# An attention and channel-mix kernel on one core: the tail tokens' load moved ahead of w_k, 82 filler products, new orders for three engines

## The chip, the core and the metric

The kernel runs on one core of one Trainium2 chip. The metric is the device time of one execution in microseconds (us). Five engines matter. TensorE (PE) multiplies and transposes into PSUM; a product is a weight load (PEld) and a matmul. ScalarE (ACT) does exponentials, relu, tanh, and many copies out of PSUM. VectorE (DVE) does the elementwise work and the other copies. GpSimd (POOL) issues the loads that cast float32 to bfloat16; SyncE (SP) issues the first loads of q, the stores of the output, and transposing DMAs. Each engine works through its own list in order and waits on semaphores for the others.

## What is computed

```python
scores = scale * q @ k.T                     # 8 batches, 8 heads, 576 tokens, head size 64
scores = where(0 <= rel < 128, scores - slope[h] * rel, -1e9)    # rel = row - column
attn   = softmax(scores) @ v
x      = attn, heads side by side            # 8 x 576 x 512
xk, xr = mu * x + (1 - mu) * x_prev          # x_prev: x one token earlier; mu_k and mu_r
k      = relu(xk @ w_k)                      # 512 x 1024
out    = sigmoid(xr @ w_r) * ((k * k) @ w_v) # 1024 x 512
```

Products take bfloat16 and add up in float32; the output is float32.

## The kernel before

**Tiles.** A batch's 576 tokens are four blocks of 128 and a tail of 64 (`LAST`). The heads go in four groups `g` of two. Batches go in pairs `P`: the channel mix runs over the 1152 tokens of a pair in four blocks, which I call a (tokens 0 to 511 of the pair, for pair 0 split into a, 0 to 255, and b, 256 to 511), c (512 to 895) and d (896 to 1151).

**The order of the work is written out.** `Plan.add` takes every operation of the program with what it needs; those of PE, ACT and DVE are numbered in the order in which the program adds them. `ORDER` (from L19) holds, for each of the three engines, the list of these numbers in which it does them. Where an operation may run on ACT or on DVE (copies of qk, some squares), the list that holds its number decides. `Plan.run` steps through a model of the machine to choose buffers and to merge all queues, but within PE, ACT and DVE the lists are followed. GpSimd's loads keep the order in which the program makes them; for batch 0, the weights and batch 1 that is the string `LOADS`, a letter for each step of `load_step`: v (the first half of batch 0's v), 2 (q and k of batch 0, tokens 256 to 511, to `part_buf`), K and k (the halves of w_k), t (the tail tokens' q and k, to `ts`, in `tail_load`, L534), V (the second half of v, and its tail `tv`), a, b, c (batch 1's q and k, its tail, its v), R (w_r), W and w (the halves of w_v).

**The operations by name.** On PE, for batch 0 and group g: Tg transposes q and k of tokens 0 to 255 (loaded by SP and ACT in float32, cast by DVE for groups 0 and 1, transposed as float32 for groups 2 and 3); Bg writes the bias into PSUM as a product (L748); Sg adds the scores (L742); Ag multiplies by v (L395); Xg transposes the attended output (L398). With a prime they belong to the second part, tokens 256 to 575; qg are its transposes of q and k, t0 those of the tail tokens (L395, `ident,ts`), M that of mu. For batch b from 1 on: qb.g, Sb.g (twice, for two halves), Ab.g, Xb.g (two groups at once), tb; the bias is there a multiplication by a mask on DVE (L779). In the mix, KPxf is the product with 128 columns of w_k for block x of pair P, RPxc that with w_r for 128 tokens, VPxc one half (four of eight parts) of that with w_v. W is a filler: a product of zeros by zeros (`emit_warm`), 90 of them (`NWARM`), which nobody reads.

Behind a T, q or t stands a copy from PSUM (L715, ACT or DVE); behind S the exponential on ACT (L766); behind A the division on DVE (L813, L819); behind X a copy on ACT (L715), then the difference and the two mixes xk and xr on DVE (L906, L913); behind K a relu on ACT (L1022) and a square on DVE or ACT (L996, L994); behind R a tanh on ACT (L1040); behind the second V the output product on DVE (L1054) and the store.

PE's list from its start to the first product of a mix after those of pair 0's blocks a and b, by these names:

```
Wx34 B3 B0 B2 Wx23 T0 Wx11 S0 T3 Wx6 B1 W T2 S3 Wx4 T1 Wx4 M A3 W S2 A0 Wx4 q1 S1 q3 A2 B3' W X3 q2 A1 S3' q0
B0' W X0 X1 B2' X2 S2' t0 S0' B0' B3' B2' S3' S0' B1' S2' B1' S1' A0' A3' S1' K0a4 A2' X0' K0a6 A1' K0a0 K0a2
K0a1 X1' q1.1 X2' K0a5 X3' K0a7 K0a3 q1.2 q1.0 S1.1 K0b5 t1 K0b1 R0a1 R0a0 S1.1 S1.0x2 V0a0 V0a1 q1.3 S1.2
V0a0 S1.2 S1.3 V0a1 S1.3 K0b3 K0b6 K0b2 A1.0 A1.2 A1.1 A1.3 K0b0 R0b2 X1.0 K0b4 q2.1 K0b7 V0b2 R0b3 q2.2 X1.2
t2 V0b3 S2.1x2 S2.2 V0b3 V0b2 q2.0 q2.3 S2.2 K0d3
```

The functions that the change touches:

Of the kernel before, what the change touches and what calls it, by code (L numbers as in the profile page):

```python
# [20 lines left out]

ORDER = {
    "PE": [int(x) for x in """
# [17 lines left out]
""".split()],  # L41
    "ACT": [int(x) for x in """
# [11 lines left out]
""".split()],  # L54
    "DVE": [int(x) for x in """
# [16 lines left out]
""".split()],  # L72
}

# [168 lines left out]
def kernel(  # L243
# [32 lines left out]
    XB = range(4, B)  # L276
    XO = range(6, B)
    X0 = 16
    NWARM = 90
    LOADS = 'v2KtVkabRWwc'  # L280
    XD = 4
    OTL = 1.5
    FIN = 384
# [328 lines left out]
    def load_step(what):  # L612
        if what in "vV":
            if what == "v" and VCUT:
                n_w["d"] = pool_op(0.55, emit_cut, [n_ident])
            for j in ((0, 1) if what == "v" else (2, 3)):
                vl[0].append(v_load(0, j, vh[0], [gv[0]] + blank_v + (
                    src0[1, VDEP - 1] if VDEP and j == 0 else [])))
                if j == 0 and not VCUT:
                    n_w["d"] = pool_op(0.55, emit_cut, [n_ident, last[POOL]])  # L620
                    last[POOL] = n_w["d"]
            if what == "V":
                vl[0].append(tv_load(0, vh[0], blank[0:4]))
        elif what in "23":
            if what == "2":
                src1[0] = src1[1] = [run_load(lambda: part_buf, i, 0, 256, 2, 0, H) for i in range(2)]
        elif what == "t":
            th[0], tl[0] = tail_load(0)
        elif what in "Kk":
            j = int(what == "k")  # L630
            n_w["k", j] = w_load(wk_sb[:, :, 512 * j:512 * j + 512],
                                 moe_w_k[:, 512 * j:512 * j + 512], 820 + 210 * (1 - j))
        elif what == "R":
            n_w["r"] = w_load(wr_sb, moe_w_r, 840)
        elif what in "Ww":
            j = int(what == "w")
            n_w["v", j] = w_load(wv_sb[:, 4 * j:4 * j + 4], moe_w_v[512 * j:512 * j + 512], 820)
        elif what in "abc":
            batch_load(1, what)
# [33 lines left out]

    for what in LOADS:
        load_step(what)
# [32 lines left out]
    g_wm = plan.add(VIR, 0.0001, 0.0001, [], (0,), None, [h_wm])  # L708
    for i in range(NWARM):
        plan.add(PE, 0.118 if i < 40 else 0.056, 0.0, [n_warm, g_wm], (1e12, i), emit_warm, (), [h_wm])  # L710
# [613 lines left out]
```

## Time and profile before

| | |
|---|---|
| time, median of 3 runs | 228.89 us (228.83 to 229.37) |
| the profiled execution | 228.23 us, span 226.2 us |
| PE busy | 218.4 us, 97% of the span |
| DVE busy | 186.3 us, 82% |
| ACT busy | 156.2 us, 69% |
| POOL busy (issuing loads) | 92.1 us, 41% |
| fillers | 90, from 1.0 to 15.6 us |
| granted PE clock | 0.998 |

The span runs from the first to the last instruction in the profile. Matmuls are pipelined, so one's length (some 0.2 us for the shortest) is longer than the time until the next can start, and PE can count as busy while it does little. A row of a timeline gives the start, the length of a run of like instructions, what they write and read, their count, and in brackets the idle time before them and what ended it. A row of the chain of waits gives start, length, engine and line. Where an engine's waits name a DMA, that load had landed just before.

### The profile page before, as it was taken

What the parts mean: (1) busy time and instruction counts of PE and PEld (TensorE: products, weight loads), DVE (VectorE), ACT (ScalarE), POOL (GpSimd) and SP (SyncE); (2) the same over time, 40 slices, a digit from 0 to 9 for tenths busy, and PEclk for the clock granted to TensorE, in tenths of its full rate; (3) what the DMA queues carried; (4) which work ended last, traced back from release to release, by engine and by line L of the source; (5) the groups of instructions that cost most, each with busy time, mean ns of one, the idle gap of its engine ahead of it and who ended that gap; (6) DMA issues with size and microseconds to landing.
All of it is one profiled execution on the core that took longest, in us unless ns stands there. A gap on an engine that the chain in (4) does not pass through costs nothing.

```text
span 226.2 us, 6452 instructions
## 1 busy us (share of the span) xinstructions
PE 218.4 (97%) x2572; PEld 132.6 (59%) x2603; DVE 186.3 (82%) x418; ACT 156.2 (69%) x284; POOL 92.1 (41%) x118
## 2 busy tenths in 40 slices
PE   8999999999999999999999999999999999999994
PEld 7766855756666555555666554556665564655442
DVE  7388979899879999988989969969989999834153
ACT  2489999899999876877497198665697644545121
POOL 8956727599971973396258610330000000000000
PEclk9999999999999999999999999999999999999999
DMA  6999999999999999999999999799811083202026
GB/s 169 180 185 199 197 195 177 224 149 155 182 171 165 98 194 173 197 170 151 206 183 128 155 188 179 155 114 239 154 31 32 36 158 64 90 3 80 17 96 229
DMA packets 129981, 33.19 MB, mean 147 GB/s; under 512 B 116632, under 2 KB 126112, under 8 KB 129952
## 3 DMA queue, kind: packets, MB, share of 16 engines
q0 software_dynamic: 95728, 16.26, 100.6%
q1 hardware_dynamic: 32480, 15.94, 33.5%
q10 hardware_dynamic: 1744, 0.59, 1.1%
q8 instruction: 20, 0.33, 0.6%
q14 instruction: 9, 0.07, 0.1%
HBM read 33.56 MB, written 9.44 MB: 190 GB/s over the span
## 4 chain that ended last, share of the span: by engine, by line
PE 78%; ACT 12%; DMA 3%; DVE 3%; issue 2%; DVEq 0%; ACTq 0%
PE duo L395 68%; PE duo L742 6%; ACT at L766 3%; PE duo L398 3%; DMA out_dram<-ot 3%; ACT qk L715 3%; ACT xt L715 2%; ACT rl L1022 2%; ACT mask L1198 1%; DVE ot L1054 1%; PE duo L748 1%; ACT kk L994 1%; DVE xu L819 1%; DVE kk L996 0%; ACT rs L1040 0%
## 5 line engine op out<-in xcount | busy, mean ns | idle before, releaser
L395 PE MATMUL duo<-xk,wk_sb 128*128 128x256 bf16 (+2 forms) x413 | 71.0, 313 | 0.5 <-ACT rl L1022 0.2
L766 ACT ACTIVATE at<-duo 128x1024 bf16<-128x1024 f32 (+2 forms) x68 | 64.4, 1008 | 8.4 <-PE duo L742 8.3
L395 PE MATMUL duo<-wv_sb,kk 128*128 128x512 bf16 (+2 forms) x279 | 68.5, 373 | 1.3 <-issue 0.6
L1022 ACT ACTIVATE rl<-duo 128x256 bf16<-128x256 f32 (+2 forms) x104 | 47.6, 499 | 26.2 <-PE duo L395 20.9
L395 PEld LDWEIGHTS <-wk_sb 128*128 128x128 bf16 x416 | 38.9, 97 | 23.8 <-issue 1.6
L779 DVE TENSOR_TENSOR at<-at,mask 128x1024 bf16<-128x1024 bf16 x56 | 37.9, 686 | 7.1 <-ACT at L766 6.7
L395 PEld LDWEIGHTS <-kk 128*128 128x128 bf16 x296 | 26.8, 98 | 27.4 <-issue 0.9
L519 POOL DMA_DIRECT2D vs<-in_v_dram x32 | 28.5, 909 | 32.5 <-PE duo L395 30.9
L996 DVE TENSOR_TENSOR kk<-rl 128x256 bf16<-128x256 bf16 (+2 forms) x92 | 29.6, 336 | 10.8 <-ACT rl L1022 10.1
L1040 ACT ACTIVATE rs<-duo 128x512 bf16<-128x512 f32 x36 | 22.3, 628 | 22.5 <-DVE ot L1054 15.1
L395 PE MATMUL duo<-wr_sb,xr 128*128 128x512 bf16 x133 | 34.9, 379 | 0.6
L1054 DVE SCALAR_TENSOR_TENSOR ot<-rs,duo 128x512 f32<-128x512 bf16 (+2 forms) x37 | 24.3, 664 | 9.3 <-PE duo L395 5.7
L819 DVE TENSOR_TENSOR xu<-duo,rc 128x640 bf16<-128x640 f32 (+2 forms) x36 | 26.6, 745 | 0.4
L913 DVE SCALAR_TENSOR_TENSOR xr<-dl,mu_sb,xt 128x576 bf16<-128x576 bf16 (+1 forms) x32 | 24.9, 779 | 0.0
L913 DVE SCALAR_TENSOR_TENSOR xk<-dl,mu_sb,xt 128x576 bf16<-128x576 bf16 (+1 forms) x32 | 24.5, 778 | 0.1
L395 PEld LDWEIGHTS <-at 128*128 128x128 bf16 x576 | 21.3, 97 | 5.5 <-issue 0.9
L395 PEld LDWEIGHTS <-xr 128*128 128x128 bf16 x144 | 13.8, 98 | 14.5 <-issue 0.4
L395 PE MATMUL duo<-vs,at 128*128 128x65 bf16 x512 | 21.8, 193 | 0.0
L550 POOL DMA_DIRECT2D cb<-in_k_dram x20 | 17.8, 930 | 4.9 <-DMA vs<-in_v_dram 4.4
L550 POOL DMA_DIRECT2D cb<-in_q_dram x20 | 17.8, 942 | 1.4 <-DMA cb<-in_k_dram 1.4
L715 ACT COPY xt<-duo 128x640 bf16<-128x640 bf16 (+3 forms) x28 | 15.6, 593 | 2.4 <-PE duo L398 2.4
L715 ACT COPY qk<-duo 128x512 bf16<-128x512 bf16 (+1 forms) x26 | 15.1, 605 | 2.6 <-PE duo L398 2.6
(73 smaller groups left out, 189.0 us busy)
## 6 DMA issues: line engine op xcount, KB each, us to landing
out_dram<-ot SPq DMA_DIRECT2D x30, 256.0 KB, 4.7
vs<-in_v_dram POOLq DMA_DIRECT2D x32, 128.0 KB, 7.9
cb<-in_q_dram POOLq DMA_DIRECT2D x20, 128.0 KB, 9.5
cb<-in_k_dram POOLq DMA_DIRECT2D x20, 128.0 KB, 10.8
out_dram<-ot SPq DMA_DIRECT2D x10, 128.0 KB, 1.8
wk_sb<-in_moe_w_k_dram POOLq DMA_DIRECT2D x2, 512.0 KB, 8.7
cb<-in_q_dram POOLq DMA_DIRECT2D x4, 256.0 KB, 8.7
cb<-in_k_dram POOLq DMA_DIRECT2D x4, 256.0 KB, 8.9
```

What stands on the lines that cost most here:

```text
L395: return use(h, nc.tensor.matmul(*a, **k))
L519: return dma(POOL, 256, issue_t(1024), lambda e: nc.gpsimd.dma_start(out=vs_buf[h.idx][:, j, :, 0:D], in_=v[b, :, 128 * j:128 * j + 128].r ...
L550: return [dma(POOL, 256, issue_t(1024), lambda e, r=r: nc.gpsimd.dma_start(out=cb_buf[h.idx][:, i, r], in_=src[:, :, r]), [g], kind="q") f ...
L715: return (nc.scalar.copy if e == ACT else nc.vector.tensor_copy)(out=out, in_=in_)
L766: lambda e, ah=ah, w=w, hp=hp: nc.scalar.activation(out=ah(), in_=two(hp)[:, :, 0:w], func=AF.Exp, scale=float(scale)), (), [hp])
L779: nc.vector.tensor_tensor(out=a, in0=a, in1=m, op=ALU.mult)
L819: use(hp, nc.vector.tensor_tensor(out=out_, in0=a5()[:, :, :, 0:D], in1=rc[:, :, 0:nt, None].to_broadcast([128, 2, nt, D]), op=ALU.mult), hx)
L913: lambda e: nc.vector.scalar_tensor_tensor(out=buf[hk.idx][:, g, e0 + c0:e0 + c1], in0=dls(), scalar=mu[:, g:g + 1], in1=xc(1), op0=ALU.mu ...
L996: nc.vector.tensor_tensor(out=out, in0=in_, in1=in_, op=ALU.mult)
L1022: a = op(ACT, act_t(n), [s], pr, lambda e, hp=hp, hr=hr: use(hp, nc.scalar.activation(out=rl_buf[hr.idx][:, 0:n], in_=one(hp)[:, 0:n], fun ...
L1040: lambda e, hp=hp, hs=hs: use(hp, nc.scalar.activation(out=rs_buf[hs.idx], in_=one(hp), func=AF.Tanh, scale=0.5), hs), [hs], [hp])
L1054: use(hv, nc.vector.scalar_tensor_tensor(out=ot_buf[ho.idx][:, a:b], in0=rs_buf[hs.idx][:, a:b], scalar=1.0, in1=one(hv)[:, a:b], op0=ALU. ...
```

## The change

Three things change. The letter t moves ahead of K in `LOADS`. `NWARM` goes from 90 to 82; since the fillers are numbered 39 to 128 before and 39 to 120 after, every later operation's number falls by 8, and nearly every number in the lists changes for that alone. And all three lists are new.

```diff
 ORDER = {
     "PE": [int(x) for x in """
-40 113 74 125 85 56 118 80 117 109 43 51 42 89 121 63 103 88 49 92 96 66 94 48 119 127 126 68 100 55 101 110 107
...
+105 79 88 117 91 107 56 92 89 98 78 102 101 66 110 49 69 104 67 58 115 53 51 114 50 84 68 93 119 57 112 87 54 99
...
     "ACT": [int(x) for x in """
-10 11 12 13 14 132 135 158 173 146 161 207 149 240 178 223 244 189 140 154 258 166 227 193 261 247 196 260 262
...
+10 11 12 13 127 14 165 153 141 170 232 233 158 132 215 199 198 219 146 202 236 205 239 185 188 222 251 255 249
...
     "DVE": [int(x) for x in """
-0 2 4 8 3 9 7 6 5 1 35 32 36 33 30 28 34 27 26 25 29 31 129 130 143 21 23 18 17 16 19 22 144 15 20 24 170 38 175
...
+0 1 4 34 30 5 28 35 27 2 33 25 36 3 32 121 122 31 29 6 135 16 18 19 136 124 23 7 138 21 9 24 26 15 162 150 8 17
...
@@ -276,8 +276,8 @@
     X0 = 16
-    NWARM = 90
-    LOADS = 'v2KtVkabRWwc'
+    NWARM = 82
+    LOADS = 'v2tKVkabRWwc'
     XD = 4
```

The new PE list by the names above, over the same stretch:

```
Wx45 T0 Wx5 B3 W B0 W T1 Wx5 S0 Wx3 T3 W T2 Wx3 B2 W S3 W S2 A0 Wx2 A3 Wx2 B1 A2 Wx2 S1 W X3 M Wx3 q3 B2' W X2
A1 X0 q2 Wx3 q0 q1 S2' W t0 W B1'x2 X1 S1' B3' S3' S1' B0' B3' S3' S0' B0' A1' B2' S0' S2' A3' K0a0 A0' X1'
K0a5 K0a3 A2' K0a7 X3' K0a4 q1.1 K0a2 X0' K0a1 X2' K0a6 q1.0 q1.3 q1.2 S1.1 t1 K0b5 K0b4 R0a1 R0a0 S1.3 S1.0
S1.2 V0a0 V0a1 S1.1 S1.0 V0a0 V0a1 S1.2 S1.3 K0b2 K0b3 K0b1 K0b7 A1.0 A1.1 K0b0 A1.3 R0b2 A1.2 X1.0 q2.1 K0b6
R0b3 V0b2 X1.2 q2.2 S2.1 V0b3 t2 S2.2 V0b2 q2.3 q2.0 V0b3 S2.1 S2.2 K0c3
```

Thirteen operations go from ACT to DVE: the copies behind T0, T1 and T2, one of the two behind q0, q1.0, q1.3 and q2.3, and the squares behind K0a2, K0a4, K0a6, K0c1, K0c6 and K0c7. Six go from DVE to ACT: one copy behind each of q1, q3, q1.3 and q2.0, and the squares behind K0b6 and K0c5. In DVE's new list the two output products of V0a stand together ahead of the masks of S1.0, S1.2 and S1.3 (second halves); in the old list one of them stood ahead of both of S1.2's and the other ahead of S1.3's. ACT's new list makes all eight exponentials of batch 0's second part before the first of the eight mask rows (L1198); the old one has four mask rows among them. The rest of the lists, to the end, is reordered in the same manner; both end with R3d8 between the parts of V3d8.

82 rows, old and new, of the table ORDER are left out of this document.

## The prediction

> **What bounds the kernel now.** I read the page first, then busy time by stretch, then the chain of waits in order of time, and last the timelines of TensorE (PE), ScalarE (ACT), VectorE (DVE) and GpSimd (POOL) over the first 55 us. Engine rows and stretches (start:end, length, busy time and count of each engine, granted clock, DMA share, GB/s):
>
> ```profile
> span 226.2 us, 6452 instructions
> PE 218.4 (97%) x2572; PEld 132.6 (59%) x2603; DVE 186.3 (82%) x418; ACT 156.2 (69%) x284; POOL 92.1 (41%) x118
> 5.00:10.00 5.00, 4.93 (x65) 3.87 (x63) 2.47 (x9) 1.45 (x3) 5.00 (x8) 1.00 1.89 182
> 10.00:20.00 10.00, 9.73 (x206) 6.33 (x202) 7.65 (x25) 9.29 (x21) 6.21 (x10) 1.00 1.58 192
> 25.00:30.00 5.00, 4.40 (x130) 3.49 (x117) 4.96 (x13) 5.00 (x16) 2.78 (x4) 1.00 1.29 207
> 30.00:52.00 22.00, 21.74 (x408) 13.19 (x412) 19.49 (x41) 20.86 (x39) 14.56 (x19) 1.00 1.91 183
> 52.00:223.00 171.00, 168.57 (x1650) 97.68 (x1675) 143.04 (x290) 113.35 (x196) 56.47 (x68) 1.00 1.29 134
> ```
>
> From 52 to 223 us PE is busy 168.57 of 171.00 us: 2.43 us of it is idle, and a new order can win no more than that there. The real room lies ahead of 30 us, where "busy" hides fillers and short tiles. There ACT is the full engine (9.29 of 10, then 5.00 of 5), with DVE at 4.96 of 5 beside it. The early steps, first from the chain of waits (start, length), then from the timelines:
>
> ```profile
> 0.99 3.32 PE duo L395 x34
> 4.31 0.98 PE duo L748 x6
> 5.29 1.28 PE duo L395 x23
> 6.57 0.24 PE duo L398 x4
> 7.47 0.34 PE duo L742 x4
> ```
> ```profile
> 7.74 0.66 PE L398 MATMUL duo<-id,qx 128*128 128x128 f32 x4
> 28.34 0.40 PE L742 MATMUL duo<-qk 64*128 64x256 bf16 x4 [0.45 <-ACT qk L715]
> 29.44 0.38 PE L398 MATMUL duo<-ident,ts 128*128 128x128 bf16 x4 [0.16 <-ACT qk L715]
> 30.09 1.89 PE L395 MATMUL duo<-wr_sb,xr 128*128 128x512 bf16 x7
> ```
> ```profile
> 7.85 0.81 ACT L766 ACTIVATE at<-duo 128x768 bf16<-128x768 f32 x1 [0.43 <-PE duo L742]
> 13.25 0.82 ACT L766 ACTIVATE at<-duo 128x768 bf16<-128x768 f32 x1
> ```
>
> The first transposes of q and k (T0) start only when 57 fillers and three bias pairs are through; the exponentials of its four groups of heads then run from 7.85 to 14.1. From there to R0a, the first w_r product at 30.09, PE twice waits for ACT's copies of qk (0.45 and 0.16): ACT's backlog sets the start of R0a. What R0a also needs is w_r itself. The load's issue, its time to landing, and what GpSimd's waits say of other loads:
>
> ```profile
> 18.14 0.81 POOL L560 DMA_DIRECT2D wr_sb<-in_moe_w_r_dram  x1
> 29.66 0.76 POOL L515 DMA_DIRECT2D cb<-in_q_dram  x1 [1.44 <-DMA wr_sb<-in_moe_w_r_dram]
> 14.59 0.74 POOL L515 DMA_DIRECT2D cb<-in_k_dram  x1 [1.87 <-DMA wk_sb<-in_moe_w_k_dram]
> 34.79 0.74 POOL L515 DMA_DIRECT2D cb<-in_q_dram  x1 [1.84 <-DMA wv_sb<-in_moe_w_v_dram]
> ```
> ```profile
> wr_sb<-in_moe_w_r_dram POOLq DMA_DIRECT2D x1, 512.0 KB, 11.2
> ```
>
> 18.14 + 11.2 = 29.3 us. So R0a starts 0.7 us behind its weights, and the loads, which follow one another in one queue, are a floor close under the present schedule.
>
> **The change, part by part.** *Tail tokens ahead of w_k.* Only the letter t moves, past K; v stands ahead of K before and after, and V, the later half of v, behind it, so the "v" of the title is no change. The tail loads and the first scores that want them:
>
> ```profile
> L534 POOL DMA_DIRECT2D ts<-in_q_dram x1: 565/565/565, 6.7 to 6.7; - x1
> DMA to landing us min/median/max: 7.7/7.8/7.9
> 16.83 0.65 PE L395 MATMUL duo<-ident,ts 64*64 64x32 bf16 x32
> 21.40 0.61 PE L395 MATMUL duo<-xk,wk_sb 128*128 128x256 bf16 x4
> ```
>
> The tails land at about 6.7 + 7.7 = 14.4 and 14.9 and are used at 16.83. In front of w_k's 512 KB they land earlier by what these take: as an estimate 2.2 to 2.6 us, the 1.44 to 1.87 us that GpSimd waits on a load of that size and its own issue of 0.75 between; so near 12. The two tails together are a quarter of that size (64 KB each), so w_k's first half is put back by 0.6 us, from just under 14.59 to some 15; its first user is at 21.40, and the 6 us between hide that. No later load changes place. Price of the move: 0; if that cover were gone, 0.6 us.
>
> *82 fillers for 90.* Fillers run only where PE has nothing else. 23 take 1.28 us, 56 ns each, so eight are 0.45 us, all of it ahead of 17 us in time that PE waits for loads or ACT anyway: 0 by itself. What counts is the place: 45 fillers now stand ahead of T0, not 57 with three bias pairs. The first 34 end at 4.31, eleven more at 4.31 + 11 x 0.056 = 4.92, so T0 ends at 5.16, not 6.81.
>
> *The head's lists.* Three qk copies of part 0 go from ACT to DVE, which has the room there (2.47 of 5 us busy). From T0's end at 5.16: twelve fillers 0.67, two bias pairs (a third of 0.98 each) 0.65, T1 0.24: S0 at 6.7 for 7.47, its exponential 0.38 later at 7.1 for 7.85. T3 can't move: its last load was issued at 2.3 and took 5.4:
>
> ```profile
> L569 ACTq DMA_DIRECT2D qx<-in_k_dram x2: 491/520/550, 1.8 to 2.3; - x2
> DMA to landing us min/median/max: 4.1/4.9/5.4
> 8.51 0.69 DVE L715 CAST qk<-duo 128x512 bf16<-128x512 f32 x1 [1.44 <-PE duo L398]
> ```
>
> That is 7.7, the 7.74 of before. T3 ends at 8.4, DVE's copy (0.69) at 9.1, S3 at 9.3; T2's copy follows at 9.8, S2 at 9.9; the exponentials (0.8 us each) at 9.7 and 10.5; A2, which stands ahead of S1, needs the second of them, so S1 comes at about 11.6 and its exponential at 12.0. It was 13.25: **1.25 us won on ACT**. ACT also hands DVE squares and copies worth about 0.8 us (counted under the second rival). So I expect the 0.45 and 0.16 us waits on ACT to go, and R0a to be held by its weights instead: at 29.45 for 30.09, **0.64 us**. Between the bounds (0: DVE's added work or ACT still holds R0a; 0.75: it starts as w_r lands at 29.34) I take nearly the whole, since 1.25 + 0.8 is three times what is needed.
>
> *From R0a to the next mix.* Up to the first product of the next mix (K0d3 before, K0c3 after) both lists hold the same products, so that start compares them:
>
> ```profile
> 34.67 0.38 PE duo L398 x32
> 36.81 1.04 PE L395 MATMUL duo<-wv_sb,kk 128*128 128x512 bf16 x4
> 37.78 0.34 PE L742 MATMUL duo<-qk 64*128 64x256 bf16 x4
> 52.39 5.48 PE duo L395 x36
> ```
>
> Before R0a the new list has done one thing more, q1.3 (0.38). PE is full from there on (21.74 of 22), so that is **0.38 us** off the rest. A change between 128-row and 64-row products costs about 0.10: four 512-column products from 36.81 at 0.216 each ((1.04 less the 0.379 us of one)/3, with 0.379 the mean of the last one's whole length) end their issue at 37.68, and the next starts at 37.78. The new list has 16 such changes here for 18 (**0.2 us**), and 40 for 38 from there to the end (0.2 lost). One floor holds: V0a's second halves need w_v at about 34.5 (GpSimd's wait until 34.79) and come at some 34.6. Of the other, v of batch 1 for the A1 products, these rows say only that it was there at 39.43; were it no earlier, most of the gain would be lost there, as PE keeps its order. The next mix starts at 52.39 - 0.64 - 0.38 - 0.2 = 51.2.
>
> *From 52 us on.* The orders of all engines differ. The trace can't show the new ones; by the idle time of the old one the bounds are 2.4 us won and, as an estimate of equal size, 2.4 lost. Distances from producer to consumer in the two PE lists (scores to A, A to X, X to K, K to V) are alike, so I take 0, less the 0.2 of the changes. The end stays: both lists close with R3d8 between the halves of V3d8.
>
> The row of a 512-column product:
>
> ```profile
> L395 PE MATMUL duo<-wr_sb,xr 128*128 128x512 bf16 x133 | 34.9, 379 | 0.6
> ```
>
> **Sum:** 0.64 + 0.38 + 0.2 - 0.2 = 1.0 us. The profiled execution took 228.23 us (span 226.2 and 2.0 around it): 227.2. It lies 0.7 below the median of the runs, 228.89; set against that, **227.9 us**.
>
> [...] The first 34 products take 3.32 us where 56 ns each would be 1.9: the early ones run at about half speed, though the granted clock reads 1.00 in every stretch. [...]
>
> **The rivals.**
> - *Hidden anyway (0.20).* ACT or DVE still holds R0a at about 30.1, or batch 1's v the A1 products at 39.4, so no more than the 0.38 of q1.3 is won: 228.5 to 228.9, within 0.3%. For it: DVE is at 4.96 of 5 from 25 us, and it now makes five squares ahead of the last xk of batch 0. Against: ACT's 1.25 us.
> - *DVE becomes the bound (0.22), the slower side.* Ahead of 40 us, beside the part-0 copies, DVE gains three squares (0.28 each), two copies of 512 columns (0.69) and one of 256 (0.42), and gives up one square, one copy of 512 and two of 256: net 0.8 us. Its list also sets both output products of V0a ahead of the last three masks, where one stood among the last four. If DVE's part-1 xk products end later than the 28.2 of now rather than earlier, these 0.8 us and 0.6 us of one product (0.68 in the row below, 0.6 apart) fall on the A1 products; less the 0.38 of q1.3 that is 1.0 lost: 229.9. It decides at the start of the first A1 product, 39.43 now.
> [...]
>
> ```profile
> 27.16 1.01 DVE L913 SCALAR_TENSOR_TENSOR xk<-dl,mu_sb,xt 128x320 bf16<-128x320 bf16 x2
> 39.43 0.62 PE L395 MATMUL duo<-vs,at 128*128 128x65 bf16 x15
> L1054 DVE SCALAR_TENSOR_TENSOR ot<-rs,duo 128x512 f32<-128x512 bf16 x35 | 23.5, 678 | 8.4 <-PE duo L395 5.7 <-PE duo L742 1.1 <-DMA out_dram<-ot 1.0
> L996 DVE TENSOR_TENSOR kk<-rl 128x256 bf16<-128x256 bf16 x40 | 10.7, 279 | 1.2 <-ACT rl L1022 0.9
> L715 DVE COPY qk<-duo 128x256 bf16<-128x256 bf16 x4 | 1.7, 418 | 0.2 <-ACT xt L715 0.2
> ```
>
> **How the numbers follow.** The forecast has 0.55, its own range 227.0 to 228.2 (0.7 to 1.9 us won: the sum, and a part of the 2.43 us of idle time). About 0.3%, 0.7 us, is what a measurement of this kernel can tell from no change: faster 0.55; within, the first and third rivals, 0.23; slower 0.22. The range goes from 226.5, the sum and over half of the late idle time, to 230.0, just past the slower rival.
>
> **What would show it.** Right: T0 at about 4.9; exponentials of part 0 ended by 12.8; R0a within 0.2 us of w_r's landing, PE waiting on that load; the first A1 product near 38.6; the next mix at 51.2; PE idle after it about 2.4 us. Wrong: R0a still behind ACT's qk copies; DVE's masks of batch 1 late behind the output products; products of 128 columns 107 ns apart after 10 us; or the gain at 51.2 there and given back by PE waits between 52 and 223, which the lists alone can't exclude.

## The result and the profile after

The changed kernel took 228.24 us (median of 9 runs, 227.59 to 228.50), the kernel before 228.87 (228.55 to 229.84) beside it: ratio 0.9962, 95% interval 0.9945 to 0.9979. Two further comparisons, in the experiments below, gave 0.9949 (0.9926 to 0.9972) and 0.9949 (0.9929 to 0.9970). So it is faster by 0.6 to 1.2 us, and the forecast of 227.9 lies 0.34 from the time measured. The time lies a little above the forecast's own range (227.0 to 228.2), between it and the first rival (from 228.5). The working behind the forecast did not hold, though: of the way points that it named ahead of 52 us the later ones failed, and a gain came where it had put none. That the number came out near is in good part luck.

The profiled execution took 227.59 us with a span of 225.8. First its engine rows, then the same five stretches as before (length, busy time and count of PE, PE's weight loads, DVE, ACT and POOL, granted clock, DMA share, GB/s):

```profile
span 225.8 us, 6424 instructions
PE 217.7 (96%) x2563; PEld 132.6 (59%) x2595; DVE 189.8 (84%) x425; ACT 153.1 (68%) x277; POOL 92.1 (41%) x118
```
```profile
5.00:10.00 5.00, 4.96 (x62) 3.69 (x61) 4.34 (x17) 0.98 (x2) 4.86 (x7) 1.00 1.84 182
10.00:20.00 10.00, 9.95 (x209) 6.59 (x210) 8.04 (x27) 7.96 (x18) 6.04 (x9) 1.00 1.59 191
25.00:30.00 5.00, 4.12 (x128) 3.32 (x127) 4.96 (x16) 5.00 (x13) 3.31 (x4) 1.00 1.34 204
30.00:52.00 22.00, 21.16 (x377) 13.39 (x382) 20.75 (x42) 21.05 (x41) 14.62 (x18) 1.00 1.91 185
52.00:223.00 171.00, 168.48 (x1657) 97.38 (x1677) 144.03 (x293) 111.79 (x193) 56.89 (x69) 1.00 1.28 136
```

Copies have moved from ACT to DVE ahead of 10 us as planned (DVE 4.34 for 2.47), but from 10 to 20 us ACT, which was nearly full, now stands idle for 2 us, and from 25 to 30 us it is as full as before. Now the way points, in TensorE's timeline of the changed kernel (start, length, operation):

```profile
5.30 0.39 PE L398 MATMUL duo<-ident,qx 128*128 128x128 bf16 x4
15.66 0.71 PE L395 MATMUL duo<-ident,ts 64*64 64x32 bf16 x32
28.85 0.40 PE L742 MATMUL duo<-qk 64*128 64x256 bf16 x4 [0.60 <-ACT rl L1022]
30.35 1.89 PE L395 MATMUL duo<-wr_sb,xr 128*128 128x512 bf16 x7
39.69 0.62 PE L395 MATMUL duo<-vs,at 128*128 128x65 bf16 x15
52.28 0.99 PE L395 MATMUL duo<-xk,wk_sb 128*128 128x384 bf16 x5
```

T0 starts 1.1 us earlier (5.30 for 6.41) and the last exponential of part 0 ends 1.0 earlier. But R0a, at 30.35, is 0.26 us *later* than before, and the next mix begins at 52.28 for 52.39. In this pair of traces the whole new head is worth 0.1 us. ACT's timeline shows where the lead goes:

```profile
12.24 0.81 ACT L766 ACTIVATE at<-duo 128x768 bf16<-128x768 f32 x1 [0.90 <-PE duo L742]
15.30 0.65 ACT L715 COPY qk<-duo 128x256 bf16<-128x256 bf16 x2 [0.56 <-DVE xk L913]
17.24 0.37 ACT L715 COPY xt<-duo 128x256 bf16<-128x256 bf16 x1 [0.58 <-PE duo L398]
17.51 4.27 ACT L766 ACTIVATE at<-duo 128x768 bf16<-128x768 f32 x7
```

ACT could start the copies of q1 (15.30) and of X1 (17.24) only 0.56 and 0.58 us after it was free: 1.14 us, as much as T0 had won (before's kernel loses 0.17 us there). From 17.2 on ACT is full until R0a, as it was before.

### The profile page after: what moved, and what is told of

Its sections match the earlier page's. It is cut to its first block, busy times and chain, and to the rows that moved or that the text cites. A ratio compares the mean times of both kernels' runs of the same rounds, so it can differ in the third digit from the quotient of the medians.

```text
span 225.8 us, 6424 instructions
## 1 busy us (share of the span) xinstructions
PE 217.7 (96%) x2563; PEld 132.6 (59%) x2595; DVE 189.8 (84%) x425; ACT 153.1 (68%) x277; POOL 92.1 (41%) x118
## 4 chain that ended last, share of the span: by engine, by line
PE 81%; ACT 13%; DVE 3%; issue 2%; DVEq 0%; ACTq 0%
PE duo L395 70%; PE duo L742 6%; ACT at L766 5%; PE duo L398 4%; ACT xt L715 2%; ACT qk L715 2%; ACT rl L1022 2%; PE duo L748 2%; ACT rs L1040 1%; DVE xr L913 1%; DVE ot L1054 1%; ACT kk L994 0%; DVE kk L996 0%; DVE dl L906 0%; DVE xu L819 0%
## 5 line engine op out<-in xcount | busy, mean ns | idle before, releaser
L766 ACT ACTIVATE at<-duo 128x1024 bf16<-128x1024 f32 (+2 forms) x68 | 63.1, 989 | 11.5 <-PE duo L742 11.3
L1022 ACT ACTIVATE rl<-duo 128x256 bf16<-128x256 f32 (+2 forms) x104 | 46.2, 477 | 35.9 <-PE duo L395 27.9
L395 PE MATMUL duo<-wv_sb,kk 128*128 128x512 bf16 (+2 forms) x280 | 67.0, 373 | 1.4 <-issue 1.0
L779 DVE TENSOR_TENSOR at<-at,mask 128x1024 bf16<-128x1024 bf16 x56 | 37.3, 682 | 2.3 <-ACT at L766 2.1
L996 DVE TENSOR_TENSOR kk<-rl 128x256 bf16<-128x256 bf16 (+2 forms) x96 | 30.4, 337 | 10.5 <-ACT rl L1022 10.3
L1054 DVE SCALAR_TENSOR_TENSOR ot<-rs,duo 128x512 f32<-128x512 bf16 (+2 forms) x37 | 24.2, 666 | 6.0 <-PE duo L395 5.0
L395 PEld LDWEIGHTS <-xr 128*128 128x128 bf16 x144 | 13.4, 97 | 13.7 <-issue 0.4
L906 DVE TENSOR_TENSOR dl<-xt 128x576 bf16<-128x576 bf16 (+1 forms) x32 | 13.4, 437 | 3.7 <-ACT xt L715 3.4
```

The lines of the kernel that those rows point to most:

```text
L395: return use(h, nc.tensor.matmul(*a, **k))
L766: lambda e, ah=ah, w=w, hp=hp: nc.scalar.activation(out=ah(), in_=two(hp)[:, :, 0:w], func=AF.Exp, scale=float(scale)), (), [hp])
L779: nc.vector.tensor_tensor(out=a, in0=a, in1=m, op=ALU.mult)
L996: nc.vector.tensor_tensor(out=out, in0=in_, in1=in_, op=ALU.mult)
L1022: a = op(ACT, act_t(n), [s], pr, lambda e, hp=hp, hr=hr: use(hp, nc.scalar.activation(out=rl_buf[hr.idx][:, 0:n], in_=one(hp)[:, 0:n], fun ...
L1054: use(hv, nc.vector.scalar_tensor_tensor(out=ot_buf[ho.idx][:, a:b], in0=rs_buf[hs.idx][:, a:b], scalar=1.0, in1=one(hv)[:, a:b], op0=ALU. ...
```

## The experiments

Twelve kernels ran, in three groups of four; those of one group share the chip and the runs of before. Lists are named as in the description of the change; "head" is everything up to the first product of the next mix (K0d3 or K0c3), "tail" what comes after.

### Which part of the lists brings the gain

Head or tail of the lists exchanged (fillers and loads go with the head):

```diff
 headB_tailA:  NWARM = 90, LOADS = 'v2KtVkabRWwc', lists of before up to K0d3's place
+              lists of after from there on
 headA_tailB:  NWARM = 82, LOADS = 'v2tKVkabRWwc', lists of after up to K0c3's place
+              lists of before from there on
```

> All three lists of the kernel before up to the first product of the mix of blocks c and d (52 us), with its 90 fillers and its order of loads; from there the changed lists. PE does the same products ahead of that point in both. Theory L (the gain comes from the lists behind 52 us, the head gives nothing): as the changed kernel, 228.1 to 228.5 us, 0.4 to 0.7 below before. Theory H (the head brings it, as the prediction had it): as before, 228.8 to 229.0 us.

> The other way round: the changed lists, 82 fillers and the changed order of loads up to 52 us, the old lists from there. Theory L: as before, 228.7 to 229.0 us. Theory H: 228.1 to 228.4 us. If the two halves only fit together, both mixtures are slower than before.

Measured: before 229.58; headB_tailA 228.48, ratio 0.9952 (0.9931 to 0.9973); headA_tailB 228.83, ratio 0.9979 (0.9959 to 0.9999). The tail alone brings the gain of the whole change or nearly that; the head alone brings less, at the edge of what can be told from nothing. Part of that is the joint's own: just behind the place where headA_tailB goes from the new lists to the old, TensorE waits for a relu, which no other profile shows:

```profile
59.06 0.64 PE L395 MATMUL duo<-ident,cb 64*128 64x64 bf16 x32 [0.58 <-ACT rl L1019]
```

That wait must not be added to what the head is worth, though: in this trace the wait on a store, which the next section describes, is missing, and from the next mix to the last V product it takes 170.37 us, as the other old tails do (170.19 to 170.49). So the 0.75 us between the medians, with an interval of 0.5 us either way, is the head's share as far as this kernel can tell, and it agrees with the 0.5 us that the profiles show below. At least as much lies where the prediction had put 0.

### What the tail wins: one wait on an output store

All profiles put side by side from the first product of the next mix on, the old tail runs to within 0.1 us alike up to R1c4 in all five profiles that have it without a joint, and then falls apart at one place: from R1c4's start to that of K1c0 it takes 1.19 (before), 1.37, 1.39 and 1.50 us in four of them and 0.86 in the fifth (before_more12, below). In before that place is this row of VectorE and this one of TensorE:

```profile
106.89 0.69 DVE L1054 SCALAR_TENSOR_TENSOR ot<-rs,duo 128x512 f32<-128x512 bf16 x1 [0.99 <-DMA out_dram<-ot]
```
```profile
109.53 0.81 PE L395 MATMUL duo<-xk,wk_sb 128*128 128x384 bf16 x4 [0.17 <-ACT rl L1022]
```

An output product wants its buffer back from a store that has not landed: that store was issued at 99.60 us and landed 7.2 us later. Masks and squares wait behind it in DVE's order, ACT's relu behind the squares (at 108.82 in before it had idled 2.08 us for DVE's kk), and TensorE's K1c0 behind the relu. In before_less12_newloads the store took longer, and the wait was 1.29 us for 0.99:

```profile
108.11 0.69 DVE L1054 SCALAR_TENSOR_TENSOR ot<-rs,duo 128x512 f32<-128x512 bf16 x1 [1.29 <-DMA out_dram<-ot]
```
```profile
110.75 0.81 PE L395 MATMUL duo<-xk,wk_sb 128*128 128x384 bf16 x4 [0.47 <-ACT rl L1022]
```

In before_more12 the same order of DVE's work ran without that wait:

```profile
107.35 0.68 DVE L1054 SCALAR_TENSOR_TENSOR ot<-rs,duo 128x512 f32<-128x512 bf16 x1
```
```profile
110.72 0.81 PE L395 MATMUL duo<-xk,wk_sb 128*128 128x384 bf16 x4
```

What differs is the output buffer. `Plan.run` takes the lowest of the five that its model holds to be free. In the four kernels with the wait it gives this product buffer 0, whose store it takes to have landed; in before_more12 twelve more fillers move the model's clock, and the product gets buffer 2. It gets buffer 2 in headA_tailB as well, whose tail lists are the same, and there too the product waits for no store.

In before_more12 the tail, from the next mix to the last V product, took 169.86 us; with the wait it took 170.19 to 170.49. With the new lists it took 169.80 to 169.91 in all eight profiles that have them, and no wait on a store stands among those of DVE. So the new tail is not shorter as such: 169.9 against 169.86. Its gain in the span is that no product gets a buffer whose store is still under way, which the old order can have too. In the traces that is worth 0.33 to 0.63 us.

A second part lies outside the span. A run's time less its span is 1.95 to 2.09 us in the executions of all kernels with the old tail (2.0 in before's profile: 228.23 and 226.2) and 1.73 to 1.85 in those with the new one (1.8: 227.59 and 225.8), whichever head stands in front: 0.24 us. Why, no run shows. Together that is 0.6 to 0.9 us; by the medians of before and headB_tailA the tail is worth 1.1 (229.58 to 228.48), with an interval of some 0.5 us either way.

### The load order by itself

```diff
 before_newloads:                     lists_oldloads:
-    LOADS = 'v2KtVkabRWwc'           -    LOADS = 'v2tKVkabRWwc'
+    LOADS = 'v2tKVkabRWwc'           +    LOADS = 'v2KtVkabRWwc'
```

> The kernel before with the tail tokens' loads ahead of w_k and nothing else. Theory Q: w_r lands 0.4 us later, at 29.8, just ahead of its first product at 30.1, which stays: 228.8 to 229.0 us, no difference. Rival: each load behind is used so soon after it lands that the 0.4 us shows: 229.2 to 229.4 us.

> The changed kernel with the tail tokens' loads back behind w_k. In the changed trace the second tail load takes 1.7 us of the queue where it took 0.35 before, and w_r lands at 29.8 for 29.4. Theory Q (the move costs the queue 1.1 us, and the tails are there in time anyway): w_r lands near 29.4 again, first w_r product up to 0.4 us earlier, time 227.9 to 228.2 us. Rival (the new lists need the tails early; they use them at 15.7 us): the scores of the second part wait for them, 228.3 to 228.8 us.

Measured: before_newloads 229.14, ratio 0.9988 (0.9966 to 1.0010): nothing that can be told from no change. lists_oldloads 228.60, ratio 0.9971 (0.9952 to 0.9990), 0.4 to 0.5 us above the changed kernel in the other groups, which these intervals don't tell apart. Theory Q's first step failed: w_r landed at 30.01 us, not near 29.4. The profile is 0.60 us longer from S1 to R0a (19.15 for 18.55), but not because the tails came late: they had landed at 15.30 and 15.65, ahead of t0 at 16.14. TensorE stopped behind the first of t0's products, here with DVE's row beside it:

```profile
16.14 0.21 PE L392 MATMUL duo<-ident,ts 64*64 64x32 bf16 x1
16.80 0.66 PE L392 MATMUL duo<-ident,ts 64*64 64x32 bf16 x31 [0.45 <-DVE qk L712]
16.33 0.41 DVE L712 COPY qk<-duo 128x256 bf16<-128x256 bf16 x1
```

The row names DVE's copy of qk, and that fits: t0 writes two PSUM buffers, and with the old order of loads the model of `Plan.run` starts t0 1.1 us later and picks for the second of them the one that this copy reads until 16.74. In the changed kernel it picks one that ACT had read before. So the two kernels differ by more than the letter t, and the 0.60 us is the price of that choice of buffer. before_newloads, to which the plan gives the same buffers as to before, is the clean comparison, and it shows neither a price nor a gain of the move.

### Does the head hang on the fillers ahead of T0?

Put side by side, the profiles with the old head showed something that I had not looked for: from T0 to S1 it takes 6.42 or 6.43 us and from T0 to the next mix 45.98, whatever the execution, while T0 itself stood at 6.41, 7.24 and 7.44 us. So twelve fillers were taken out in front of it, and twelve put in; the same was done to the new head with ten.

```diff
 before_less12:  W x34 B3 B0 B2 W x23 T0   ->  W x34 B3 B0 B2 W x11 T0
 before_more12:  W x34 B3 B0 B2 W x23 T0   ->  W x34 B3 B0 B2 W x35 T0
 after_less10:   W x45 T0                  ->  W x35 T0
 after_again, after_third:  the changed kernel as it is
```

> The kernel before without 12 of the 23 filler products directly ahead of T0 (78 instead of 90). Theory F (the old head hangs on T0, and T0 on the queue of 57 fillers and three bias pairs): in three profiles with the old head T0 stood at 6.41, 7.24 and 7.44 us, and the first product of the next mix 45.98, 45.99 and 45.98 us later; 12 fillers at 0.056 us take 0.67 off T0 and, as long as the third and fourth loads of q and k (7.4 to 8.4) do not come last, off everything behind it: 0.3 to 0.7 us, ratio 0.997 to 0.9985. My prediction's rival (fillers ahead of T0 are worth 0 by themselves, since what counts comes later): ratio 1.000. [...]

> The kernel before with 12 filler products more directly ahead of T0 (102 instead of 90): the suspected cost the other way round, where no load can take its place. Theory F (the old head hangs on T0): T0 0.67 us (12 x 0.056) later at the same half-rate phase, the first product of the next mix 45.98 us behind T0 as in the three profiles with the old head and its 90 fillers, time 0.5 to 0.8 us more, ratio 1.002 to 1.0035. My prediction's price (a filler ahead of T0 is worth 0 by itself): ratio 0.999 to 1.001.

> The changed kernel without 10 of the 45 fillers ahead of T0 (72 instead of 82). Theory N (the new head hangs on the landing of the fourth load of q and k, 8.04 to 8.40 in three profiles, after which the mix starts 44.2 to 44.6 us later): nothing changes against the changed kernel, ratio 0.999 to 1.001 of it, T0 about 0.2 to 0.6 us earlier and the mix not. Rival (T0 still carries the head): 0.2 to 0.5 us less.

> The changed kernel itself, for the pair with the others of this call. In its profile T0 stands at 5.30 us when the half-rate fillers end at 4.79. If the new head hangs on the fourth load of q and k (landing 8.04) and not on the fillers, then in this profile, whatever the half-rate phase lasts, the first product of the next mix stands 44.2 to 44.5 us after that landing; if it hangs on T0, 46.98 us after T0. Time 0.997 of before or a little less.

> The changed kernel again, for the pair with the others of this call: ratio 0.994 to 0.9965. Its first product of the next mix 21.93 us behind R0a as in all five profiles with the new lists up to 52 us, S1 to R0a 18.55 or 18.63, the last V of the last part 169.8 to 169.9 us behind the next mix; T0 between 4.7 and 5.8, as the half-rate phase falls.

Measured: before_less12 229.30 against 229.25, ratio 0.9998 (0.9979 to 1.0017); before_more12 229.52 against 229.20, ratio 1.0014 (0.9992 to 1.0036); after_less10 227.98 (0.9943, 0.9922 to 0.9965) beside after_again 228.09 (0.9949, 0.9926 to 0.9972); after_third 228.08 (0.9949, 0.9929 to 0.9970). For the old head the times bear out neither theory. The profiles say why: both steps of theory F hold, T0 stands 0.64 us earlier in before_less12 than in headB_tailA, whose half-rate phase (the stretch of early products that start 107 ns apart, for the 56 of later ones) is alike (6.60 for 7.24), and 0.58 later in before_more12 (7.82), and S1 follows 6.42 or 6.43 behind it each time; but something else pays for it. In before_less12 a stop of TensorE of 0.23 us follows behind S1 and has grown to 0.44 by R0a, and the store's wait is longer (1.17 us). In before_more12 the store's wait is gone by the other choice of buffer, which gives back 0.33 us or more of the 0.67.

Why T0 moves from one execution to the next is seen in the chain of waits, first headB_tailA, then before_more12, each with the fillers, the bias pairs, the fillers behind them and T0:

```profile
0.99 3.81 PE duo L391 x34
4.80 1.32 PE duo L744 x6
6.12 1.28 PE duo L391 x23
7.40 0.24 PE duo L394 x4
```
```profile
0.99 3.81 PE duo L395 x34
4.80 1.22 PE duo L748 x6
6.03 1.95 PE duo L395 x35
7.98 0.24 PE duo L398 x4
```

In before's profile the first 34 products took 3.32 us and the bias pairs 0.98: 25 of the 34 started 107 ns apart, the others 56. Here all 34 are 107 apart, and the first bias pairs at half rate too (0.64 us each for 0.325). The half-rate phase ended at 3.6 us in before's profile (4.8 in the changed kernel's), at about 5.2 to 5.8 in five others with the old head, and at 6.7 in best_try. The trace from which I predicted was the luckiest of seven.

The new head is not so exposed. With T0 at 4.54 to 5.30 S1 starts 3.70 to 3.76 us behind the landing of the last of the first four pairs of loads (after, after_third, after_less10, after_t0late); with T0 at 5.77 (after_again) it waits for T0 and comes 4.17 behind. In headA_tailB and lists_oldloads, with T0 at 5.51 and 5.57, S1 comes 4.06 and 3.88 us behind the landing, and what held it there is open. The chain of after_third, whose T0 was at 4.80, goes back to the load of q of that pair, which landed at 7.84 (that of k at 8.18):

```profile
2.27 5.57 DMA qx<-in_q_dram
7.88 0.68 PE duo L398 x3
8.59 0.69 DVE qk L715
```

So after_less10 did as theory N said: T0 at 4.54, and the time the same. The next mix started at 52.28, 52.36, 52.75 and twice 52.77 in the five profiles with the new head and its loads (after_t0late left out), and at 52.39, 53.23 and 53.42 in those with the old head and its 90 fillers. In the pair of before and after the difference was 0.1 us; between the medians of the two sets it is 0.5.

### Fewer fillers and the load move together, and a mixture of all that helped

```diff
 before_less12_newloads:  before_less12 with LOADS = 'v2tKVkabRWwc'
 best_try:                the same up to K0d3's place, lists of after from there on
```

> The kernel before without 12 of the 23 fillers directly ahead of T0, and with the tail tokens and v ahead of w_k. Without the load move the 12 fillers alone brought 0.9998: T0 stood 0.64 us earlier than in the profile with the same half-rate phase (6.60 for 7.24), but S1 to R0a took 17.70 instead of 17.26 us, and in that profile the tail tokens of k landed at 16.55, 0.7 ahead of t0. Theory FL (the tail tokens' landing took the place of T0): with the move they land at 12.4 to 14.3, S1 to R0a is 17.26 again, ratio 0.996 to 0.998. Rival (something else holds the head as soon as T0 is earlier, such as the landing of the fourth load of q and k at 7.7 to 8.8): 0.9985 to 1.0005, S1 to R0a 17.26 and T0 to S1 above 6.43.

> The old lists up to 52 us without 12 of the 23 fillers ahead of T0, the new lists behind it, the new order of the loads. By the parts: lists behind 52 us 0.45 us (stretch 169.8 to 169.9 instead of 170.2 to 170.4), fillers and move together 0.3 to 0.8 if theory FL holds: ratio 0.993 to 0.9955, level with the changed kernel or up to 0.3 us below it. If only the lists behind 52 us count: 0.996 to 0.998.

Measured: before_less12_newloads 229.04 against 229.20, ratio 0.9994 (0.9973 to 1.0015); best_try 228.22, ratio 0.9962 (0.9943 to 0.9980), and the changed kernel beside them 228.08. Theory FL falls: the tails landed at 11.91 and 12.25, yet S1 to R0a took 18.00 us, more than the 17.70 without the move. What the two profiles share is not a landing but TensorE's stop at the same place, in front of X2, of 0.23 and 0.52 us. The row of before_less12_newloads names ACT's copy of xt, but by the plan X2's buffer had last been read by ACT's copy of q0, which ended at 16.43, so that no producer explains the stop:

```profile
17.05 0.28 PE L398 MATMUL duo<-ident,xu 128*128 128x128 bf16 x2 [0.35 <-ACT xt L715]
```

Nothing that I tried beats the changed kernel by more than its interval: after_less10 came out 0.1 us below it, best_try 0.1 above.

### Is it ACT's order that gives the lead back?

From S1 to R0a the new lists take 18.54 to 18.63 us and the old ones 17.25 to 17.27, in every profile without one of TensorE's stops or a changed order. To move X1's copy away from ACT's 0.58 us of waiting, t0 was set behind X1 and the first chunks of S1', S3' and S0'. The plan's choice of PSUM buffers changed with it, so this is not the order alone:

```diff
 PE:   S2' W                         X1 S1' B3' S3'
-      t0 W B1' B1' X1 S1' B3' S3' S1' B0' B3' S3' S0' B0'
+      B1' X1 S1' B3' S3' B0' S0' t0 W B1' S1' B3' S3' B0'
 ACT:  exponentials of S0' (first chunk) ahead of S1' and S3' (second); DVE: the copies behind t0 after three more steps
```

> The changed kernel with one piece of the list of TensorE between 15.6 and 19 us put otherwise: the transposes of the tail tokens (t0) behind X1 and the first chunks of S1, S3 and S0 of the second part, ScalarE's exponentials and VectorE's two copies of the tail tokens in the same order. Theory A (ScalarE's order gives the head's gain back: its copy xt1 waits 0.58 us for X1 at 17.24, which stands behind t0, with seven exponentials behind it): xt1 at 16.5, the last exponential of the second part 0.4 to 0.7 us earlier, R0a at 29.7 to 30.0 instead of 30.35, the time 0.3 to 0.6 us less than the changed kernel. Rival (VectorE or the landing of w_r at 29.3 to 30.0 holds R0a as well): below 0.2 us.

Measured: 229.45, ratio 1.0012 (0.9990 to 1.0034): 1.36 us slower than the changed kernel beside it. ACT's timeline in that stretch, and DVE's row of the copies behind t0:

```profile
16.68 0.37 ACT L715 COPY xt<-duo 128x256 bf16<-128x256 bf16 x1
16.95 2.21 ACT L766 ACTIVATE at<-duo 128x768 bf16<-128x768 f32 x3
20.49 1.15 ACT L766 ACTIVATE at<-duo 128x512 bf16<-128x512 f32 x2 [1.32 <-PE duo L742]
22.17 1.08 ACT L766 ACTIVATE at<-duo 128x512 bf16<-128x512 f32 x2 [0.53 <-PE duo L742]
19.41 0.76 DVE L715 CAST tt<-duo 128x256 bf16<-128x256 f32 x2 [2.08 <-ACT at L766]
```

The first step came as expected (the copy at 16.68 for 17.24), but the second chunks of the scores need the tails' copies, which now came at 19.41, and ACT idled 1.85 us for those instead of 0.58. Their row names an exponential of ACT, 0.5 us after t0's last product had ended (18.90); why they wait for that is open. R0a went to 31.95. So that wait was not loose play in ACT's order: t0, the copies behind it and the exponentials form a chain of their own through three engines, and putting t0 behind the first chunks lengthens it. That ACT's 1.14 us of idling are the reason why S1 to R0a takes 1.3 us longer is argued from the traces, not shown; the one other order tried here did not remove it.

## Why the prediction was right, and where it was wrong

- **T0's end at 5.16 for 6.81** (it ended at 5.68 for 6.81): the step was sound, its size rested on "the first 34 end at 4.31". They do so in that one execution; in the changed kernel's own, 35 fillers started 107 ns apart instead of 25. In the two other profiles with the old head and its 90 fillers the old T0 lies 0.8 and 1.0 us later than I took it to be, so the head is worth more to the median than to the trace.
- **ACT's 1.25 us**: S1 came at 11.80 (forecast about 11.6) and its exponential at 12.24 (12.0): 1.0 won.
- **R0a at 29.45, held by w_r**: this is the step that failed. ACT's waits for qk went, but TensorE then waited 0.60 for ACT's relu, and R0a came at 30.35, 0.55 behind w_r's landing (29.80). I had carried ACT's lead of 1.25 through the order of the old list; the new one sets ACT idle 1.14 us on the way. The first rival, "hidden anyway", described this.
- **0.38 for q1.3 and 0.2 for fewer changes of 128 and 64 rows**: R0a to the next mix took 21.93 or 21.94 us with the new lists and 22.29 or 22.30 with the old (22.40 once), 0.37 won. That is q1.3 alone; of the 0.2 nothing is to be seen. (The division in the working gives 0.220 us for a product, not 0.216; it takes 0.01 from the 0.10 and decides nothing.)
- **The next mix at 51.2**: 52.28, and up to 52.77 in other executions.
- **From 52 us on, 0 less 0.2**: wrong by its sign. 0.28 us came in the profiled pair up to the last V product. The cause stood in a row that I quoted for another purpose: L1054's waits end with "<-DMA out_dram<-ot 1.0". I had counted idle time of TensorE by the stretch (2.43 us) and taken the rest for alike, without asking which of DVE's waits end in TensorE's.
- **"2.0 around it"**: I carried the time outside the span over unchanged. It is 1.8 us with the new tail: 0.24 of the profiled pair's 0.64.
- **The load move at 0**: held in before_newloads. w_k's first half landed at 16.37 in the profile after, for 14.31, put back by 2.1 us and not 0.6, still well ahead of its first product at 21.08. That the move can change the plan's choice of buffers I had not thought of.
- **A filler at 0 by itself**: right for the time, by no merit: in the old head each filler ahead of T0 moves T0 and S1, and other waits then take its place, or the store's wait goes.
- **The slower rival, and the sign of 107 ns**: DVE's added work didn't hold the first A1 products by 1.0 (39.69 for 39.43, all of it R0a's lateness). Nor were the fillers 107 ns apart after 10 us: three in a row at 12.50 us took 0.34 and one alone 0.22, so they were about 60 ns apart. The granted clock, 1.00 in all five stretches, can't say so, since it also reads 1.00 from 1 to 3 us, where they were 107 apart.

So the sum, 1.0 us, came out near the truth by luck: a head that was 1.1 us too good (51.2 for 52.28) was made up for by a tail, a time outside the span and a half-rate phase that I hadn't priced.

## What to carry to other kernels

Ask of every wait on a store or load in an engine's list who stands behind it, even if it is one wait of 1 us in 226: here one output buffer, given out again while its store was under way, made TensorE's time depend on when that store landed (a wait of 0.99 us on it in before, 1.29 in before_less12_newloads, and 0.17 and 0.47 us of TensorE's in front of K1c0). Where a program chooses its buffers by a model, a change of order, of fillers or of loads also changes that choice: compare the buffers before a difference is put down to the order. A profile is one execution: before a way point in it is used as a constant, look at what may vary ahead of it, such as the end of TensorE's half-rate phase. And an earlier start is worth only what the next full engine can use (here T0's 1.1 us were 0.1 at the next mix); compare way points at which both orders have done the same products.

## What the runs showed of the hardware

- **The half-rate phase ended between 3.6 us (before) and 6.7 us (best_try)** after the span's start, with the first product at 0.99 each time. In before and in the changed kernel 128-column products started 107 ns apart from there up to 3.63 and 4.70 us, and 56 ns apart behind it; the 384-column bias pairs that fell into the phase in other profiles took 0.64 us for 0.325. What sets its end, no run shows.
- **Outside of a few places the program repeated itself to 0.01 us** (from R0a to the next mix 21.93 or 21.94 us with the new lists, 22.29 or 22.30 with the old ones). Between S1 and the next mix, and from there to the end, the same lists with the same buffers gave the same distances but for the store's wait, the stops below and a few steps of 0.1; so differences of 0.2 us between traces can be read.
- **The store on which the output product waited took 6.2 to 7.5 us from its issue to its landing**; all stores of before took 1.7 to 8.2, 3.0 in the median. This one was issued at 99.60 us in before and ended the wait at 106.79; in the three other kernels with the wait it took 7.4 to 7.5 us, and in before_more12 the same store took 6.2.
- **TensorE stopped three times at the same count of instructions.** In before_less12 (0.54 us between two weight loads) and before_less12_newloads (0.83, where 0.31 is usual at that place) it stopped in front of X2, in after_less10 (0.16, where 0.05 is usual) within t0: each time behind 223 weight loads and 223 products, in two different lists, and no producer explains it. My reading is that the supply of instructions ran short there. The first 16 KB packet of the instruction queue behind 8 us started at 14.5, 14.7 and 14.0 us in these three profiles, and the next weight load came 2.2 to 2.4 us behind that start. In the eleven others the packet started at 11.4 to 13.7 and the 224th weight load came 3.1 to 5.0 us behind it. All four kernels with 72 or 78 fillers have a late packet (13.7 to 14.7), the ten others one at 11.4 to 12.9: so it may be what pays for fewer fillers. That the packet is the cause is argued, not shown.
